# A linear-attention layer fused with a feed-forward layer: one step becomes a 64-token chunk of two batches, with column halves alternating on TensorE and elementwise work taken off GpSimd

## The chip, the cores and the metric

The kernel runs on one core of one Trainium2 chip. Its time is the device time of one execution, in microseconds (us). A core has TensorE (PE in the profile; PEld is its loading of stationary weights), VectorE (DVE), ScalarE (ACT), GpSimd (POOL) and SyncE (SP, which here only starts transfers). Each runs its own instructions in the order in which they were emitted and waits on semaphores for the others.

## The reference

Attention with a decaying state (B = 4 batches, H = 8 heads, S = 768 tokens, head size D = 48), then a feed-forward layer on the 3072 tokens of 384 features, with 2048 hidden features and the gate h * tanh(softplus(h)):

```python
    state = np.zeros((B, H, D, D), dtype=np.float32)
    for t in range(S):
        kt, vt, rt = (k[:, :, t], v[:, :, t], r[:, :, t])
        cur = np.einsum('bhd,bhe->bhde', u[None] * kt, vt)
        y[:, :, t] = np.einsum('bhd,bhde->bhe', rt, state + cur)
        state = w[None, :, :, None] * state + np.einsum('bhd,bhe->bhde', kt, vt)
...
    h = x @ w_in
    sp = np.where(h > 20.0, h, np.log1p(np.exp(np.minimum(h, 20.0))))
    g = h * np.tanh(sp)
    return (g @ w_out).astype(np.float32)
```

The two feed-forward weights arrive as float64.

## The kernel before

**Attention.** The recurrence is done in chunks of C = 64 tokens. A step `s` is two chunks (index `c`) of one batch for all heads; there are 24 steps, six a batch. Heads go in four pairs (`p`) of an even and an odd head (`par`). For a step `load_step` and `load_v` fetch r, k and v; `scale` multiplies r and k by powers of w (L365, L374, into `G`), `diag` makes the u term (L385, L389, L394, L400), `keys` the decayed keys (L418, into `KI`). `scores` multiplies r by k (L435, tile `pa`), and `attend` puts the masked scores into `G` (L459). `chunk` then does, for one chunk, the output y (L496, tile `yt`) and the state for the next chunk (L505, tile `st`), which L518 copies from PSUM into `Wt`, where v lies. So chunk 1 needs chunk 0's state, and a step needs that of the step before it, except at the start of a batch. Each loop over `p` writes y into one half of the output rows (`c * C`), and a state product into rows 0 to 47 or 64 to 111. `finish` copies y out (L527), transposes it (L548) and splits it into two parts of few bits, `xh` and `xl` (L539, L541).

**Weights.** There are 16 tiles of 128 x 768 float64 weights. `convert` makes float32 of their bits (L296 to L312; L312 is an integer add on POOL) and splits the result into two parts (L318, L320).

**Feed-forward.** The tokens go in 8 groups of three steps (384 tokens). For each of 16 f-tiles (128 hidden features) of a group, `up` does 9 matmuls into tile `hp` and `down` 9 into `acc`, all at L572. The `hp` tiles are copied out (L669), and four together form a batch: sigmoid, arctan and sin on ACT (L602 to L608), then gate and split (L613 on DVE, L616 on ACT, L619 on DVE), two f-tiles at a time. Down of a tile follows `LAG` = 9 tiles behind its up. At the end of a group three tiles are copied out (L638) and stored.

**Order.** A planner (`Flow`) emits the instructions. Every piece of work is a generator that says which engines its next instruction may go to and how long it would take there, and the planner sends it where it would be ready first. `dve`, `pool`, `act` and `pe` are its costs. The attention of group g is put into the feed-forward of group g - 1: `place` gives the f-tile behind which a step's four pieces (scores, chunk 0, chunk 1, transposes) may come. Where the plan leaves PE idle, `keep_warm` inserts matmuls on zeros.

Of the kernel before, what the change touches and what calls it, by code (L numbers as in the profile page):

```python
# [23 lines left out]
C = 64  # L24
ST = 2 * C
NST = S // ST
# [25 lines left out]
LAG = 9  # L52
LO0, HI0, LO1, HI1 = 0.05, 0.9, 0.1, 0.75
# [3 lines left out]
# how much a microsecond of an engine counts, and when the engines and tables are there for the stream  # L57
COST = dict(dve=2)
# [67 lines left out]
def dve(cols, fast=False):  # L126
    return {"dve": 0.067 + cols / (1920 if fast else 960)}


def pool(cols):  # L130
    return {"pool": 0.13 + cols / 470}


def act(cols):
    return {"act": 0.03 + cols / 1120}
# [7 lines left out]
def rwkv_mish_kernel(ctx, tc, rkT, rkN, vN, wT, uN, w_in, w_out, consts, rkF, vF, wF, uF, outT):  # L143
# [29 lines left out]
    # persistent double buffers, of which some rows stay zero  # L173
# [7 lines left out]
    for par in range(2):  # L181
        nc.gpsimd.memset(Wt[0][DROWS[par], par, 0], 0.0)
# [6 lines left out]
    # powers of w: TR[., i] = w^(i-32), TK[., j] = w^(31-j), TKn[j, .] = w^(95-j)  # L189
# [53 lines left out]
    doubled(nc.gpsimd, TR, slice)  # L243
# [4 lines left out]
    engines = {"dve": nc.vector, "pool": nc.gpsimd}  # L248
# [3 lines left out]
    def check_range():  # L252
        # whether every w is in the range of these tables
# [17 lines left out]
    # A slot holds a tile of weights as it comes, float64, or its two parts.  # L271
# [10 lines left out]
    def convert(c):  # L282
        """Float64 weights as float32, rounded to nearest, from their bits: the upper word gives
        sign, exponent and 20 bits; the lower one is added to them as a number. Then the two parts."""
        v = nc.vector
        yield f"raw{c}"
        if c >= WE_BUFS:
            yield f"half{c - WE_BUFS}"
        raw = raws.pop(c)
        up, low = raw[:, :, 1], raw[:, :, 0]  # L290
        x, r = up.bitcast(F32), low.bitcast(F32)
# [3 lines left out]
        if engine == "act":  # L295
            nc.scalar.activation(e, x, AF.Abs)  # L296
# [5 lines left out]
        v.tensor_scalar(out=eu, in0=eu, scalar1=3, scalar2=None, op0=ALU.logical_shift_left)  # L302
        yield dve(WE)
        v.scalar_tensor_tensor(out=up, in0=up, scalar=0x80000000, in1=eu, op0=ALU.bitwise_and, op1=ALU.bitwise_xor)
        engine = yield {**act(WE), **dve(WE, True)}
        if engine == "act":
            nc.scalar.activation(r, low, AF.Copy, bias=2.0, scale=2.0**-51)
        else:
            v.tensor_scalar(out=r, in0=low, scalar1=2.0**-51, scalar2=2.0, op0=ALU.mult, op1=ALU.add)
        flow.set(f"half{c}")  # L310
        yield {"pool": 2.1}
        nc.gpsimd.tensor_tensor(out=up.bitcast(I32), in0=up.bitcast(I32), in1=low.bitcast(I32), op=ALU.add)  # L312
        flow.set(f"whole{c}")
# [4 lines left out]
        nc.scalar.copy(out=w[:, 0], in_=x)  # L318
        engine = yield {**dve(WE), **pool(WE)}
        engines[engine].tensor_tensor(out=w[:, 1], in0=x, in1=w[:, 0].bitcast(F32), op=ALU.subtract)  # L320
# [4 lines left out]
    NS = B * NST  # L325
# [4 lines left out]
    def load_step(s):  # L330
        b, i = divmod(s, NST)
# [6 lines left out]
        nc.sync.dma_start(rk[:112], rkT[b, i])  # L338
# [3 lines left out]
        nc.sync.dma_start(n, rkN[b, i])  # L342
# [3 lines left out]
    def load_v(s):  # L346
        b, i = divmod(s, NST)
        if s >= 2:
            yield f"state{s - 2}"
        yield {"sp": 0.55}  # L350
        for par in range(2):
            nc.sync.dma_start(Wt[s % 2][TROWS[par], par], vN[b, i, par])
        if i == 0 and s:
            for par in range(2):
                yield {"pool": 0.2}
                nc.gpsimd.memset(Wt[s % 2][DROWS[par], par, 0], 0.0)
        flow.set(f"v{s}")

    def scale(s):
# [4 lines left out]
        engine = yield {**pool(512), **dve(512)}  # L364
        engines[engine].tensor_tensor(  # L365
# [3 lines left out]
        if s >= 2:  # L369
            yield f"x{s - 2}"  # L370
        for par in range(2):
            r = DROWS[par]
            engine = yield {**pool(512), **dve(512)}
            engines[engine].tensor_tensor(  # L374
# [4 lines left out]
    def diag(s):  # L379
# [4 lines left out]
        engine = yield {**pool(384), **dve(384)}  # L384
        engines[engine].tensor_tensor(  # L385
            out=t1, in0=t1, in1=un.unsqueeze(1).broadcast_to([128, 2, NP, D]), op=ALU.mult
        )
        engine = yield {**pool(384), **dve(384)}
        engines[engine].tensor_tensor(out=t1, in0=t1, in1=n[:, 1], op=ALU.mult)  # L389
# [5 lines left out]
        if s >= 2:  # L395
            yield f"x{s - 2}"
        for par in range(2):
            r = TROWS[par]
            engine = yield {**pool(410), **dve(512)}
            engines[engine].tensor_tensor(  # L400
# [7 lines left out]
    def keys(s):  # L408
# [4 lines left out]
        if s >= 2:  # L413
            yield f"state{s - 2}"
        for par in range(2):
            r = TROWS[par]
            engine = yield {**pool(384), **dve(384)}
            engines[engine].tensor_tensor(  # L418
# [25 lines left out]
    def attend(s):  # L444
        q = s % 2
        yield f"scaled{s}"
        if s:
            yield f"masked{s - 1}"
            if s > GROUPS[0]:
                yield f"state{s - 1}"  # L450
        yield from paced(s, 0)
        yield pe(1.3)
        pa = scores(s)
        flow.set(f"scores{s}")
        yield f"diag{s}"
# [9 lines left out]

    def outputs(s):
        yield f"masked{s}"
# [7 lines left out]
        for c in range(2):  # L475
            yield from paced(s, 1 + c)
            yield from chunk(s, c)
        flow.start(finish(s), rank(s) - L_FIN)

    ys = {}  # L480

    def chunk(s, c):
        q = s % 2
        early = s < GROUPS[0]
        last = c == 1 and s % NST == NST - 1
        yield pe(0.4 if last else (1.35, 0.9)[c])
        if c == 0:
            y = ps.tile([128, 512], F32, name="yt", tag="yt")
            st = [ps.tile([128, 512], F32, name="st", tag=f"{'acc' if early else 'pa'}{par}") for par in range(2)]
            ys[s] = y, st  # L490
        y, st = ys[s]
        for par in range(2):
            k = slice(0, (128, 112)[par])
            for p in range(NP):
                h = 2 * p + par
                nc.tensor.matmul(  # L496
                    y[c * C : (c + 1) * C, h * D : (h + 1) * D],
                    lhsT=G[q][k, par, c, p, :],
                    rhs=Wt[q][k, par, c, p, :],
                    start=True,  # L500
                    stop=True,
                )
            if not last:
                for p in range(NP):
                    nc.tensor.matmul(  # L505
                        st[par][DROWS[par], p * D : (p + 1) * D],
                        lhsT=KI[q][k, par, c, p, :],
# [4 lines left out]
        if not last:  # L512
            nq, ncx = (q, 1) if c == 0 else ((s + 1) % 2, 0)
            for par in range(2):
                r = DROWS[par]
                src = st[par][r, : NP * D].rearrange("d (p e) -> d p e", e=D)
                engine = yield {**act(200), **dve(200)}
                (nc.scalar.copy if engine == "act" else nc.vector.tensor_copy)(out=Wt[nq][r, par, ncx], in_=src)  # L518
        if c == 1:
            flow.set(f"state{s}")  # L520

    def finish(s):
        g = group[s]
        y = ys.pop(s)[0]
        yield act(384)
        ysb = G[s % 2][:, 1].rearrange("a c p i -> a (c p i)")[:, :DM]
        nc.scalar.copy(out=ysb, in_=y[:, :DM])  # L527
        flow.set(f"y{s}")
        if s == starts[g]:
# [360 lines left out]
```

## Time and profile before

| | |
|---|---|
| median of 3 runs | 609.29 us (609.12 to 612.25) |
| profiled execution | span 608.9 us from the first to the last instruction; the page gives no other time for it, and the nearest run is 0.2 us longer |
| TensorE busy | 564.8 us (93%) |
| weight load busy | 534.2 us (88%) |
| VectorE busy | 392.7 us (64%) |
| ScalarE busy | 395.5 us (65%) |
| GpSimd busy | 209.2 us (34%) |
| mean granted TensorE clock | 0.954 |
| moved | HBM 37.98 MB read, 4.72 MB written |

A busy engine is not yet a bound: the shares are means over stages. The slices and stretches shown below say when each engine is full. In the timeline rows stand the start, the time, the engine, the line, the operation, the tile written and those read, shapes, and a count. In the groups stand a line's busy time, the mean of one instruction in ns, and the idle time of the engine ahead of them with what ended it.

### The profile page before, as it was taken

How to read it: one execution, taken by the hardware profiler on the slowest of the kernel's cores; microseconds unless marked ns; L12 is line 12 of the kernel's file. 1: busy time of each engine (PE TensorE's matmuls, PEld its weight loads, DVE VectorE, ACT ScalarE, POOL GpSimd, SP SyncE). 2: the span in 40 equal slices, each digit the busy share in tenths (PEclk: the TensorE clock that was granted, in tenths of full speed). 3: DMA queues.
4: the chain of work that ended last, by engine and by line, in shares of the span. 5: the costliest groups of instructions: out<-in, count | busy, mean ns of one | idle time of the engine just before them, and what ended most of it. 6: DMA issues, size and time to landing. Idle time of an engine off the chain costs nothing. (4 is left out here: it accounts for less than half of the span.)

```text
span 608.9 us, 11432 instructions
## 1 busy us (share of the span) xinstructions
PE 564.8 (93%) x4810; PEld 534.2 (88%) x4810; DVE 392.7 (64%) x502; ACT 395.5 (65%) x478; POOL 209.2 (34%) x167
## 2 busy tenths in 40 slices
PE   7778767779899999999999999999999999999994
PEld 5667766669799999999999999999999999999994
DVE  5999989999768346754756376736684465132332
ACT  4456774648665874766766775587467757678871
POOL 6655588665654113420336033403332120000000
PEclk8798858889799999999999999999999999999998
DMA  8893512011123012301131022302230101000101
GB/s 245 294 373 119 160 57 64 20 57 49 35 70 110 1 57 71 109 14 57 44 105 46 1 70 78 100 2 70 71 103 7 58 15 40 1 0 2 40 0 44
DMA packets 16620, 43.53 MB, mean 71 GB/s; under 512 B 2352, under 2 KB 8752, under 8 KB 16560
## 3 DMA queue, kind: packets, MB, share of 16 engines
q1 hardware_dynamic: 12800, 37.76, 19.6%
q10 hardware_dynamic: 3760, 4.95, 2.3%
q8 instruction: 40, 0.66, 0.4%
q14 instruction: 20, 0.16, 0.1%
HBM read 37.98 MB, written 4.72 MB: 70 GB/s over the span
## 5 line engine op out<-in xcount | busy, mean ns | idle before, releaser
L572 PE MATMUL hp<-xh,w 128*128 128x384 f32 x768 | 225.7, 350 | 2.2 <-DVE hb L669 2.2
L572 PE MATMUL acc<-gh,w 128*128 128x384 f32 x768 | 220.6, 343 | 0.3 <-ACT gh L616 0.3
L572 PEld LDWEIGHTS hp<-xh,w 128*128 128x128 f32 x768 | 143.8, 192 | 5.2 <-DVE hb L669 2.6
L572 PEld LDWEIGHTS acc<-gh,w 128*128 128x128 f32 x768 | 142.8, 191 | 1.9 <-ACT gh L616 0.7
L572 PE MATMUL hp<-xl,w 128*128 128x384 f32 x384 | 131.3, 342 | 2.0 <-DVE xl L541 2.0
L572 PE MATMUL acc<-gl,w 128*128 128x384 f32 x384 | 130.6, 340 | 0.5 <-DVE gl L619 0.5
L669 ACT COPY hb<-hp 128x384 f32<-128x384 f32 x99 | 47.1, 476 | 84.1 <-PE hp L572 83.5
L496 PEld LDWEIGHTS yt<-Wt,G 128*64 128x64 f32 (+1 forms) x768 | 55.2, 147 | 37.0 <-issue 13.4
L613 DVE TENSOR_TENSOR hb<-hb,fa 128x768 f32<-128x768 f32 x64 | 66.3, 1060 | 32.3 <-ACT fa L608 32.3
L496 PE MATMUL yt<-Wt,G 128*64 128x48 f32 (+1 forms) x768 | 63.6, 235 | 23.9 <-DVE G L459 9.9
L572 PEld LDWEIGHTS hp<-xl,w 128*128 128x128 f32 x384 | 74.1, 193 | 2.3 <-DVE xl L541 2.3
L572 PEld LDWEIGHTS acc<-gl,w 128*128 128x128 f32 x384 | 73.4, 191 | 0.8 <-DVE gl L619 0.8
L616 ACT CAST gh<-hb 128x768 fp32r<-128x768 f32 x64 | 51.9, 836 | 33.4 <-DVE hb L613 33.3
L385 POOL TENSOR_TENSOR rkn<-rkn,un 128x384 f32<-128x384 f32 x17 | 20.1, 1182 | 155.0 <-DMA rkn<-in_rkN_dram 155.0
L619 DVE TENSOR_TENSOR gl<-hb,gh 128x768 fp32r<-128x768 f32 x64 | 65.5, 1046 | 10.3 <-ACT gh L616 9.6
L669 DVE COPY hb<-hp 128x384 f32<-128x384 f32 x29 | 16.1, 556 | 65.3 <-PE hp L572 65.2
L400 POOL TENSOR_TENSOR G<-cst,sd 64x512 f32<-64x512 f32 x35 | 46.6, 1331 | 21.0 <-PE t L548 11.0
L505 PE MATMUL st<-Wt,KI 112*48 112x48 f32 (+1 forms) x704 | 51.0, 219 | 0.0
L602 ACT ACTIVATE fa<-hb,bias_ln 128x1536 f32<-128x1536 f32 x32 | 50.5, 1579 | 0.4
L608 ACT ACTIVATE fa<-fa 128x1536 f32<-128x1536 f32 x32 | 47.6, 1487 | 0.4
L605 ACT ACTIVATE fa<-fa 128x1536 f32<-128x1536 f32 x32 | 47.6, 1488 | 0.3
L608 ACT ACT_TABLE_LOAD x32 | 41.1, 1283 | 0.9 <-ACT ob L638 0.4
(70 smaller groups left out, 691.0 us busy)
## 6 DMA issues: line engine op xcount, KB each, us to landing
rk<-in_rkT_dram SPq DMA_DIRECT2D x24, 448.0 KB, 4.1
rkn<-in_rkN_dram SPq DMA_DIRECT2D x24, 384.0 KB, 4.5
wraw<-in_w_in_dram SPq DMA_DIRECT2D x8, 768.0 KB, 8.8
wraw<-in_w_out_dram SPq DMA_DIRECT2D x8, 768.0 KB, 6.8
Wt<-in_vN_dram SPq DMA_DIRECT2D x48, 96.0 KB, 2.4
out_dram<-ob ACTq DMA_DIRECT2D x24, 192.0 KB, 1.9
cst<-in_consts_dram ACTq DMA_DIRECT2D x1, 128.0 KB, 4.7
un<-in_uN_dram ACTq DMA_DIRECT2D x2, 48.0 KB, 4.6
```

Of the source, the lines that this page charges most:

```text
L385: engines[engine].tensor_tensor(out=t1, in0=t1, in1=un.unsqueeze(1).broadcast_to([128, 2, NP, D]), op=ALU.mult)
L400: engines[engine].tensor_tensor(out=G[q][r, par], in0=ident2[r].unsqueeze(1).broadcast_to([C, 2 * NP, C]).rearrange("j (c p) i -> j c p i" ...
L496: nc.tensor.matmul(y[c * C : (c + 1) * C, h * D : (h + 1) * D], lhsT=G[q][k, par, c, p, :], rhs=Wt[q][k, par, c, p, :], start=True, stop=True,
L505: nc.tensor.matmul(st[par][DROWS[par], p * D : (p + 1) * D], lhsT=KI[q][k, par, c, p, :], rhs=Wt[q][k, par, c, p, :], start=True, stop=True,)
L572: nc.tensor.matmul(out, lhsT=a, rhs=m, start=first and n == 0, stop=last and n == 2)
L602: nc.scalar.activation(o.g, o.hb, AF.Sigmoid, bias=bias_ln2, scale=1.0)
L605: nc.scalar.activation(o.g, o.g, AF.Arctan)
L608: nc.scalar.activation(o.g, o.g, AF.Sin, scale=2.0)
L613: nc.vector.tensor_tensor(out=o.hb[:, j], in0=o.hb[:, j], in1=o.g[:, j], op=ALU.mult)
L616: nc.scalar.copy(out=o.gh[:, j], in_=o.hb[:, j])
L619: nc.vector.tensor_tensor(out=o.gl[:, j], in0=o.hb[:, j], in1=o.gh[:, j].bitcast(F32), op=ALU.subtract)
L669: (nc.scalar.copy if engine == "act" else nc.vector.tensor_copy)(out=o.hb[:, j], in_=h)
```

## The change

- **Steps.** A step is now one chunk of two batches (`i, q = divmod(s, NQ)`): index `c` in the tiles is the batch of the pair. Steps s and s + 1 are independent; s + 2 needs the state of s.
- **Products.** `outputs` does all y products of a step, with `c` innermost, so that output rows 0 to 63 and 64 to 127 alternate; then all state products into one PSUM tile, with `par` innermost, so that rows 0 to 47 and 64 to 111 alternate. One copy for each `par` (384 columns) takes the state into `Wt`, where there were two of 192.
- **Insertions.** A step has two pieces instead of four. The transposes of step s - 1 go ahead of the scores of step s (`joined`), except at the ends of groups.
- **GpSimd** keeps memsets. `scale`, `diag`, `keys`, the integer add, the weight split and the table TR go to DVE. The conversion works in the buffer `e` rather than in the raw tile, and a tile starts when the split two tiles earlier is done; the conversion of the low word is always on ACT.
- **Planner.** `LAG` 9 becomes 8; the costs of DVE, ACT and PE and the places of the pieces change.

Lines move by up to ten in the changed file: y is L484, the state L497, its copy L510, the transposes L550, the feed-forward L574, the integer add L307, the weight split L314, `xl` L543, the gate L615 and L621.

```diff
-LAG = 9
-LO0, HI0, LO1, HI1 = 0.05, 0.9, 0.1, 0.75
+LAG = 8
+LO0, HI0, LO1, HI1 = 0.05, 0.9, 0.05, 0.8
...
-    doubled(nc.gpsimd, TR, slice)
+    doubled(nc.vector, TR, slice)
...
         if c >= WE_BUFS:
-            yield f"half{c - WE_BUFS}"
+            yield f"split{c - WE_BUFS}"
...
+        yield act(WE)
+        nc.scalar.activation(r, low, AF.Copy, bias=2.0, scale=2.0**-51)
         yield dve(WE)
-        v.scalar_tensor_tensor(out=up, in0=up, scalar=0x80000000, in1=eu, op0=ALU.bitwise_and, op1=ALU.bitwise_xor)
...
-        yield {"pool": 2.1}
-        nc.gpsimd.tensor_tensor(out=up.bitcast(I32), in0=up.bitcast(I32), in1=low.bitcast(I32), op=ALU.add)
+        v.scalar_tensor_tensor(out=eu, in0=up, scalar=0x80000000, in1=eu, op0=ALU.bitwise_and, op1=ALU.bitwise_xor)
+        yield dve(WE)
+        v.tensor_tensor(out=e.bitcast(I32), in0=e.bitcast(I32), in1=r.bitcast(I32), op=ALU.add)
...
-            engine = yield {**pool(512), **dve(512)}
-            engines[engine].tensor_tensor(
+            yield dve(512)
+            nc.vector.tensor_tensor(
                 out=G[q][r, par], in0=rk[r, 0], in1=TR[r].unsqueeze(1).broadcast_to([D, 2, NP, C]), op=ALU.mult
             )
...
+        joined = s and group[s] == group[s - 1] and group[s]
+        if joined:
+            yield f"y{s - 1}"
         yield from paced(s, 0)
-        yield pe(1.3)
+        yield pe(1.6 if joined else 1.25)
+        t = turned(s - 1) if joined else None
         pa = scores(s)
...
-        for c in range(2):
-            yield from paced(s, 1 + c)
-            yield from chunk(s, c)
...
+        for p in range(NP):
+            for par in range(2):
+                k = slice(0, (128, 112)[par])
                 h = 2 * p + par
+                for c in range(2):
                     nc.tensor.matmul(
+                        y[c * C : (c + 1) * C, h * D : (h + 1) * D],
+                        lhsT=G[q][k, par, c, p, :],
                         rhs=Wt[q][k, par, c, p, :],
...
         if not last:
+            for c in range(2):
+                for p in range(NP):
+                    for par in range(2):
+                        k = slice(0, (128, 112)[par])
+                        n = (c * NP + p) * D
+                        nc.tensor.matmul(
+                            st[DROWS[par], n : n + D],
...
-        at = (4 * (s - starts[g]) + piece) / (4 * GROUPS[g])
+        at = (2 * (s - starts[g]) + piece) / (2 * GROUPS[g])
```

PE in the dense part, before, from the last up matmuls ahead of chunk 0 of a step to the first down matmuls behind it (an instruction here is one matmul of the program):

```order
L572 MATMUL hp<-xl,w 128x384
L572 MATMUL hp<-xh,w 128x384
L496 MATMUL yt<-Wt_88,G_86 64x48 x4
L505 MATMUL st<-Wt_88,KI_90 48x48 x4
L496 MATMUL yt<-Wt_88,G_86 64x48 x4
L505 MATMUL st<-Wt_88,KI_90 48x48 x4
L572 MATMUL acc_1765<-gh,w 128x384
```

PE in the same part after the change, from the last down matmuls ahead of a step's outputs to the first up matmuls behind them:

```order
L574 MATMUL acc_1754<-gl,w 128x384
L574 MATMUL acc_1754<-gh,w 128x384
L484 MATMUL yt<-Wt_88,G_86 64x48 x16
L497 MATMUL st<-Wt_88,KI_90 48x48 x16
L574 MATMUL hp<-xh,w 128x384
L574 MATMUL hp<-xl,w 128x384
```

Before, a second insertion of the same four rows follows one down block later; now all 32 products of a step stand in one place.

POOL before, early in the program, with the conversion of weights and the preparation of steps 3 to 5:

```order
L312 TENSOR_TENSOR wraw<-wraw 128x768 x2
L374 TENSOR_TENSOR G_86<-rk,TR 48x512
L418 TENSOR_TENSOR KI_90<-rkn,TKn 64x384
L400 TENSOR_TENSOR G_86<-cst,sd 64x512
L374 TENSOR_TENSOR G_85<-rk,TR 48x512
L385 TENSOR_TENSOR rkn<-rkn,un 128x384
L374 TENSOR_TENSOR G_85<-rk,TR 48x512
L389 TENSOR_TENSOR rkn<-rkn 128x384
L320 TENSOR_TENSOR w<-wraw,w 128x768
```

DVE after the change in the like place, up to the split of a weight tile (`ISA` is the integer add, over 1536 half-words):

```order
L407 TENSOR_TENSOR KI_90<-rkn,TKn 64x384
L305 SCALAR_TENSOR_TENSOR we<-wraw,we 128x768
L383 TENSOR_REDUCE sd<-rkn 128x8
L307 ISA we<-wraw,we 128x1536
L543 TENSOR_TENSOR xl<-t,xh 128x3x128
L453 COPY_PREDICATED G_85<-cst,pa_878 64x512
L314 TENSOR_TENSOR w<-we,w 128x768
L453 COPY_PREDICATED G_85<-cst,pa_879 64x512
L363 TENSOR_TENSOR G_86<-rk,TR 48x512
L389 TENSOR_TENSOR G_86<-cst,sd 64x512
L363 TENSOR_TENSOR G_86<-rk,TR 48x512
L389 TENSOR_TENSOR G_86<-cst,sd 64x512
```

What POOL did beside DVE stands now in DVE's own queue, between the masks (L453) that PE waits for and the splits that up tiles wait for.

More of the change, by code (lines that the diff above doesn't have):

```diff
@@ L24 @@
 C = 64
+NQ = B // 2
+NC = S // C
+NS = NC * NQ
 ST = 2 * C
-NST = S // ST
 DM, DFF = H * D, 2048
@@ L56 @@
 DMA_LAT = 2.0
-COST = dict(dve=2)
+COST = dict(dve=1.5)
 FREE = dict(pe=10.0, act=9.0, dve=7.9, pool=9.0, sp=0.5)
@@ L180, in rwkv_mish_kernel @@
             nc.gpsimd.memset(a[i][32:64, 0], 0.0)
-    for par in range(2):
-        nc.gpsimd.memset(Wt[0][DROWS[par], par, 0], 0.0)
+    for i in range(2):
+        for par in range(2):
+            nc.gpsimd.memset(Wt[i][DROWS[par], par], 0.0)
     ET = mybir.EngineType
@@ L346, in load_v @@
     def load_v(s):
-        b, i = divmod(s, NST)
+        i, q = divmod(s, NQ)
         if s >= 2:
-            yield f"state{s - 2}"
+            yield f"out{s - 2}"
         yield {"sp": 0.55}
         for par in range(2):
[L352 to L356, printed above, removed]
+            nc.sync.dma_start(Wt[q][TROWS[par], par], vN[i, q, par])
         flow.set(f"v{s}")
@@ L383, in diag @@
         t1 = n[:, 0]
-        engine = yield {**pool(384), **dve(384)}
-        engines[engine].tensor_tensor(
+        yield dve(384)
+        nc.vector.tensor_tensor(
             out=t1, in0=t1, in1=un.unsqueeze(1).broadcast_to([128, 2, NP, D]), op=ALU.mult
         )
-        engine = yield {**pool(384), **dve(384)}
-        engines[engine].tensor_tensor(out=t1, in0=t1, in1=n[:, 1], op=ALU.mult)
+        yield dve(384)
+        nc.vector.tensor_tensor(out=t1, in0=t1, in1=n[:, 1], op=ALU.mult)
         if s >= 2:
@@ L413, in keys @@
         if s >= 2:
-            yield f"state{s - 2}"
+            yield f"out{s - 2}"
         for par in range(2):
             r = TROWS[par]
-            engine = yield {**pool(384), **dve(384)}
-            engines[engine].tensor_tensor(
+            yield dve(384)
+            nc.vector.tensor_tensor(
                 out=KI[q][r, par],
@@ L464, in attend @@
         flow.set(f"masked{s}")
+    ys = {}
     def outputs(s):
+        q = s % 2
+        early = s < GROUPS[0]
+        last = s >= NS - NQ
         yield f"masked{s}"
@@ L474, in outputs @@
                 yield f"x{s - 1}"
-        for c in range(2):
-            yield from paced(s, 1 + c)
-            yield from chunk(s, c)
[L478 to L494, printed above, removed]
-                h = 2 * p + par
[L496 to L504, printed above, removed]
+        yield from paced(s, 1)
+        yield pe(1.1 if last else 2.0)
+        y = ps.tile([128, 512], F32, name="yt", tag="yt")
+        st = ps.tile([128, 512], F32, name="st", tag="acc0" if early else "pa0")
+        for p in range(NP):
+            for par in range(2):
+                k = slice(0, (128, 112)[par])
+                h = 2 * p + par
+                for c in range(2):
                     nc.tensor.matmul(
-                        st[par][DROWS[par], p * D : (p + 1) * D],
-                        lhsT=KI[q][k, par, c, p, :],
+                        y[c * C : (c + 1) * C, h * D : (h + 1) * D],
+                        lhsT=G[q][k, par, c, p, :],
                         rhs=Wt[q][k, par, c, p, :],
@@ L512, in chunk, with evacuate_y, turned, finish @@
         if not last:
-            nq, ncx = (q, 1) if c == 0 else ((s + 1) % 2, 0)
+            for c in range(2):
+                for p in range(NP):
+                    for par in range(2):
+                        k = slice(0, (128, 112)[par])
+                        n = (c * NP + p) * D
+                        nc.tensor.matmul(
+                            st[DROWS[par], n : n + D],
+                            lhsT=KI[q][k, par, c, p, :],
+                            rhs=Wt[q][k, par, c, p, :],
+                            start=True,
+                            stop=True,
+                        )
+        flow.set(f"out{s}")
+        flow.start(evacuate_y(s, y), rank(s) - L_FIN)
+        if not last:
             for par in range(2):
                 r = DROWS[par]
[L516 to L524, printed above, removed]
+                engine = yield {**act(384), **dve(384)}
+                (nc.scalar.copy if engine == "act" else nc.vector.tensor_copy)(
+                    out=Wt[q][r, par].rearrange("d c p e -> d (c p e)"), in_=st[r, : 2 * NP * D]
+                )
+        flow.set(f"state{s}")
+    def evacuate_y(s, y):
+        if s:
+            yield f"turned{s - 1}"
         yield act(384)
-        ysb = G[s % 2][:, 1].rearrange("a c p i -> a (c p i)")[:, :DM]
+        ys[s] = ysb = G[s % 2][:, 1].rearrange("a c p i -> a (c p i)")[:, :DM]
         nc.scalar.copy(out=ysb, in_=y[:, :DM])
         flow.set(f"y{s}")
+        if s + 1 == NS or group[s + 1] != group[s] or not group[s]:
+            yield from paced(s, 2)
+            yield pe(0.36)
+            flow.start(finish(s, turned(s)), rank(s) - L_FIN)
+    def turned(s):
+        t = transposes(ys.pop(s), "acc2" if s < GROUPS[0] else "yt")
+        flow.set(f"turned{s}")
+        return t
+    def finish(s, t):
+        g = group[s]
         if s == starts[g]:
@@ L713, in down_tile @@
                 for mt in range(KT):
-                    yield f"out{g - 1},{mt}"
+                    yield f"put{g - 1},{mt}"
             else:
@@ L730, in output @@
         put(engine, mt, T, slice(starts[g] * 128, starts[g] * 128 + T))
-        flow.set(f"out{g},{mt}")
+        flow.set(f"put{g},{mt}")
     def ffn():
```

78 lines of the change are left out of this document (36 added, 42 removed).

## Prediction

> **What bounds the kernel now.** I read the page first: which engine is full, and when.
>
> ```profile
> PE 564.8 (93%) x4810; PEld 534.2 (88%) x4810; DVE 392.7 (64%) x502; ACT 395.5 (65%) x478; POOL 209.2 (34%) x167
> ...
> PE   7778767779899999999999999999999999999994
> ...
> DVE  5999989999768346754756376736684465132332
> ...
> POOL 6655588665654113420336033403332120000000
> ```
>
> There are two regimes. From about slice 10 (a slice is 15.2 us) TensorE (PE) is full; before that PE has gaps and VectorE (DVE) is full, with GpSimd (POOL) busy beside it. The stage view puts numbers on both.
>
> ```profile
> 0.00:50.00 50.00, 38.33 (x420) 31.50 (x420) 42.78 (x64) 23.53 (x47) 29.98 (x35) 0.84 0.85 298
> 50.00:100.00 50.00, 37.12 (x272) 34.02 (x272) 46.74 (x55) 31.67 (x38) 36.64 (x21) 0.81 0.28 85
> 100.00:141.50 41.50, 32.43 (x290) 29.90 (x290) 40.19 (x45) 24.15 (x34) 28.39 (x21) 0.89 0.18 53
> 300.00:400.00 100.00, 100.00 (x914) 95.36 (x913) 62.59 (x83) 66.03 (x80) 32.56 (x27) 1.00 0.22 66
> ```
>
> After the stretch come PE, weight load, DVE, ACT and POOL busy time, the granted clock, and DMA. Up to 141.5 us DVE is busy for 42.78 + 46.74 + 40.19 = 129.7 us; from 300 to 400 PE never stops and DVE has 37 us to spare. I cut at 141.5 because there the second group's feed-forward starts (its first matmul is the second row below):
>
> ```profile
> 141.29 0.34 PE L572 MATMUL acc<-gh,w 128*128 128x384 f32 x1
> 141.46 0.34 PE L572 MATMUL hp<-xh,w 128*128 128x384 f32 x1
> ...
> 601.43 0.34 PE L572 MATMUL acc<-gh,w 128*128 128x384 f32 x1
> ```
>
> The last matmul ends at 601.43 + 0.34 = 601.8, and the span is 608.9: a tail of 7.1 us for three copies and their stores. So span = 141.5 (DVE's regime) + 460.3 (PE's) + 7.1. I predict each part.
>
> **PE's regime: what an insertion costs.** In the timeline of PE, an inserted piece of attention costs the distance between the last feed-forward matmul before it and the second one behind it, less two normal steps. [...]
>
> ```profile
> 264.31 0.33 PE L572 MATMUL hp<-xl,w 128*128 128x384 f32 x1
> ...
> 282.68 0.34 PE L572 MATMUL acc<-gh,w 128*128 128x384 f32 x1
> 282.95 1.15 PE L435 MATMUL pa<-G,rk 48*64 48x64 f32 x32
> 284.03 0.45 PE L572 MATMUL hp<-xh,w 128*128 128x384 f32 x1
> 284.31 0.34 PE L572 MATMUL hp<-xl,w 128*128 128x384 f32 x1
> ...
> 288.65 0.34 PE L572 MATMUL hp<-xh,w 128*128 128x384 f32 x1
> 288.91 0.67 PE L496 MATMUL yt<-Wt,G 128*64 128x48 f32 x8
> 289.42 0.52 PE L505 MATMUL st<-Wt,KI 128*48 128x48 f32 x8
> ...
> 290.07 0.22 PE L496 MATMUL yt<-Wt,G 112*64 112x48 f32 x1
> 290.09 0.21 PE L505 MATMUL st<-Wt,KI 112*48 112x48 f32 x1
> 290.13 0.22 PE L496 MATMUL yt<-Wt,G 112*64 112x48 f32 x1
> ...
> 290.79 0.33 PE L572 MATMUL acc<-gl,w 128*128 128x384 f32 x1
> ...
> 292.00 0.34 PE L572 MATMUL acc<-gh,w 128*128 128x384 f32 x1
> ...
> 294.00 0.34 PE L572 MATMUL hp<-xl,w 128*128 128x384 f32 x1
> ```
>
> The normal step: from 264.31 to 282.68 lie 106 steps, 173.3 ns each, so a block of nine takes 1.56 us. Scores: 284.31 - 282.68 - 0.35 = 1.28 us for 32 matmuls (the program's 16, each of two passes). They start over 284.03 - 282.95 = 1.08 us, 34 ns apiece; the other 0.2 us is the price of inserting at all. Chunk 0: 290.79 - 288.65 - 0.35 = 1.79 us. Chunk 1: 294.00 - 292.00 - 0.35 = 1.65 us. So y and state cost 3.44 us a step.
>
> Why so much, the rows inside chunk 0 tell. Eight y that write one column half take 289.42 - 288.91 = 0.51 us, 64 ns each. Where y (rows 0 to 63 of its output) and the odd state product (64 to 111) alternate, a pair takes 290.13 - 290.07 = 0.06 us, about 28 ns apiece. Two column halves run beside each other, although both use the same 112 contraction rows.
>
> The change alternates halves in every y and every state product: 64 matmuls in one insertion. At 28 ns that is 1.8 + 0.2 = 2.0 us; at the scores' 34 ns, 2.4. I take 2.0, since the 28 ns are those of these very products. Its open point: in the quoted pair the two outputs lie in different PSUM tiles, now in one (all y in yt, all state in pa0), which no row shows. If that undoes the overlap, 64 times 64 ns + 0.2 = 4.3 us is the upper bound.
>
> [...]
>
> Behind 141.5 us lie 18 steps: before, 18 x 1.79 + 15 x 1.65 + 3 batch ends of 16 y alone (16 x 64 ns + 0.2 = 1.2) = 60.6 us. After, 16 x 2.0 + 2 final steps of y alone (32 x 28 ns + 0.2 = 1.1) = 34.2 us. **Saved: 26.4 us.** Scores and transposes keep their matmuls; joining them in 12 places could save at most 12 x 0.2 = 2.4 us and is taken as nothing.
>
> **LAG 8.** One down block lies ahead of the second group's start instead of behind it: minus 1.6 us here, and plus 1.6 at the end, where the last gating chain is covered by five down blocks instead of six. Net zero.
>
> **Lost time in PE's regime.** 460.3 us less 233 blocks x 1.56 (363.4), 60.6 and 18 x (1.28 + 0.33 for transposes) = 29.0 leaves 7.3 us lost before. PE misses 0.9 us of it in one stretch at the end (next row), where the last gate is awaited. For after I take 6: the end 0.9 + 1.6 = 2.5, the rest 3.5. What could grow is the gating chain:
>
> ```profile
> 590.00:600.00 10.00, 9.12 (x51) 8.54 (x50) 3.65 (x4) 4.11 (x4) 0.00 (x0) 1.00 0.01 2
> ```
>
> ```profile
> 273.38 1.82 DVE L619 TENSOR_TENSOR gl<-hb,gh 128x768 fp32r<-128x768 f32 x2 [0.78 <-ACT gh L616]
> 276.61 0.34 PE L572 MATMUL hp<-xh,w 128*128 128x384 f32 x1
> ```
>
> This gate ends at 275.2, and the up tile that reuses its buffer starts at 276.6: 1.4 us to spare where no large insertion covers it. A group has one such place after the change too, and six groups that are 2 us late each would lose 12 us. DVE's load does not force it: a group's 3 steps need, by the prices below, 15 x 0.69 + 15 x 0.55 + 3 x 0.55 + 6 x 0.73 + 16 gates x 0.95 + 5 copies x 0.55 = 43 us of about 61 (32 blocks, 3 x 3.6 of attention).
>
> **DVE's regime: GpSimd's work at DVE's price.** Two groups of the same gate, first up to 141.5 us, then from 500 to 600 where POOL is idle:
>
> ```profile
> L613 DVE TENSOR_TENSOR hb<-hb,fa 128x768 f32<-128x768 f32 x6 | 8.1, 1383 | 0.0
> ...
> L613 DVE TENSOR_TENSOR hb<-hb,fa 128x768 f32<-128x768 f32 x14 | 12.8, 952 | 15.5 <-ACT fa L608 15.5
> ```
>
> Beside a working POOL the same instruction takes 1383 ns instead of 952. POOL's 95 us up to 141.5 were thus partly paid by DVE. The clean prices stand in a stretch with POOL idle, and in one at 113 us:
>
> ```profile
> 113.92 0.69 DVE L374 TENSOR_TENSOR G<-rk,TR 48x512 f32<-48x512 f32 x1
> ...
> 136.60 0.95 DVE L304 SCALAR_TENSOR_TENSOR wraw<-wraw,we 128x768 uint32<-128x768 uint32 x1
> 137.47 0.55 DVE L385 TENSOR_TENSOR rkn<-rkn,un 128x384 f32<-128x384 f32 x1
> 137.94 0.55 DVE L300 TENSOR_SCALAR we<-we 128x768 f32<-128x768 f32 x1
> 138.41 0.55 DVE L389 TENSOR_TENSOR rkn<-rkn 128x384 f32<-128x384 f32 x1
> ```
>
> In the new order DVE has, up to the split of step 5 (L543, which opens the second group): 37 products of 512 columns x 0.69 = 25.5; 38 of 384 x 0.55 = 20.9; 25 of 768 x 0.95 = 23.8; 14 three-operand ones x 0.95 = 13.3; 33 single-input ones x 0.55 = 18.2; 12 masked copies x 0.73 = 8.8; 8 reductions and 3 PSUM copies x 0.55 = 6.1; 26 table and other small ones, about 4; and 13 integer adds (L307), new on DVE. For their price the program gives 1536 half-words; as 768 words an add costs 0.95 like its neighbours, and at one half-word a cycle, by the slope from 0.69 (512) to 0.95 (768), about 1.75. I take 0.95, 12.4 us, because the instruction has the byte count of a 768-column one; the other end adds 10.4.
>
> The sum is 133 us. Instructions that are queued start 0.47 apart though they last 0.55 (the three rows above); half of some 200 gaining 0.06 to 0.08 takes off 6. DVE's first table operation can start at about 6.5 us, as now. Without waits the split comes at 133.5. Waits are what DVE hardly has now (129.7 busy of 141.5). When it is faster it will meet ACT and PE: the masks behind the scores of the first steps, the first gate behind four feed-forward tiles and three activations, the gates of the next batches. I put 9 us on it, bounded by 3 and 18. **Start of the second group: 143 us (before 141.5); 137 to 152, with dear adds to 160.** The tables' extra doubling (TR on DVE, 7 small ones) is in the sum; the four memsets on POOL are early and hide behind the first loads; SP's loads keep their number and their bytes; ACT's six more word conversions hide, as ACT is busy 24 to 32 us of 50.
>
> **The sum**: 608.9 + 1.5 (start) - 26.4 - 1.6 (block moved ahead) - 1.3 (lost 7.3 to 6) = 581.1. The median of the runs, 609.29, is 0.4 above this span: **581.5, rounded to 582 us.**
>
> **Rivals.**
> 1. The adds run one half-word a cycle, or ACT holds DVE up for 18 us: start at 152 to 154, 591 to 593 us. For it: no row shows the add on DVE. Against: ACT is half idle there.
> [...]
> 3. The chain with 1.4 us to spare breaks: 2 us in each of six groups, 594 us.
> 4. The early regime really shrinks (waits of 3): 576 us; with a cheaper join, 573.
>
> The change may also not do what it says on POOL; the order shows only memsets left there, so I give that nothing.
>
> [...]
>
> **How the numbers follow.** Likeliest case 0.58, by itself 576 to 588; rival 1 0.16; rival 2 0.06; rival 3 0.10; rival 4 0.08; both 1 and 3 or worse, 600 to 612, 0.02. The range goes from the lower end of rival 4 to the upper of 1 and 3 with the 34 ns pace (16 x 0.4 = 6 us more): 572 to 599, leaving out about 0.12. About 0.5% (3 us) is what a measurement here can tell from none. Faster 0.92, same 0.02, slower 0.06.
>
> **What would show it.** Right: in PE's timeline y and state in one stretch of some 1.8 us; DVE's gates at 0.95 us from the start; the second group's first up tile near 143 us; PE full from there. Wrong: y starts 60 ns apart (rival 2); L307 at 1.7 us (rival 1); PE idle ahead of up tiles with DVE's gl as releaser (rival 3). A start after 160 us, or several us lost in each group, would break the forecast.

## The result and the profile after

| | median | runs | against before |
|---|---|---|---|
| before | 610.02 us | 609.12 to 612.25 (4) | |
| after | 583.07 us | 582.20 to 588.28 (4) | 0.957, 95% interval 0.952 to 0.961 |

The change makes the kernel 27 us faster. The forecast was 582 us, range 572 to 599. The profiled execution took 582.2 us with a span of 580.3.

The page of the kernel after: totals, then slices (now 14.5 us each).

```profile
PE 525.2 (90%) x4825; PEld 500.8 (86%) x4825; DVE 388.0 (67%) x594; ACT 406.5 (70%) x490; POOL 4.2 (1%) x15
...
PE   7994473876999999999999999999999999999994
...
DVE  5996998899878755775577558846875654324332
...
POOL 2000000000000000000000000000000000000000
```

PE has lost 40 us of busy time with about as many matmul records (4825 for 4810). Of these, 30 us lie behind the start of the second group's feed-forward (456.9 us busy before, 426.7 now), where the same work overlaps more. The two regimes remain. The stretches of the kernel after (columns as before):

```profile
0.00:50.00 50.00, 44.01 (x542) 36.95 (x542) 42.02 (x89) 21.68 (x44) 4.24 (x15) 0.97 0.95 332
50.00:100.00 50.00, 21.43 (x240) 19.02 (x241) 43.48 (x68) 29.70 (x35) 0.00 (x0) 0.65 0.27 74
100.00:141.50 41.50, 29.86 (x222) 27.34 (x220) 36.51 (x55) 27.48 (x35) 0.00 (x0) 0.85 0.09 26
300.00:400.00 100.00, 100.00 (x940) 96.70 (x939) 66.35 (x98) 75.30 (x88) 0.00 (x0) 1.00 0.20 63
```

Up to 141.5 us DVE is busy for 122.0 us: less than the 129.7 of before, although all of POOL's products and adds are now its own. Groups of DVE up to 145 us show why:

```profile
L307 DVE CUSTOM_DVE_ANT_0 we<-wraw,we 128x1536 uint16<-128x1536 uint16 x14 | 13.1, 951 | 0.3 <-ACT wraw L303 0.2
...
L615 DVE TENSOR_TENSOR hb<-hb,fa 128x768 f32<-128x768 f32 x6 | 5.6, 954 | 1.4 <-ACT fa L610 1.4
```

The integer add costs 951 ns, and the gate has fallen from 1383 to 954 ns. The timeline of PE around an insertion in the dense part, and the start of the second group's feed-forward:

```profile
144.67 0.34 PE L574 MATMUL hp<-xh,w 128*128 128x384 f32 x1
...
248.52 0.34 PE L574 MATMUL acc<-gh,w 128*128 128x384 f32 x1
248.79 1.14 PE L484 MATMUL yt<-Wt,G 128*64 128x48 f32 x32
249.76 0.89 PE L497 MATMUL st<-Wt,KI 128*48 128x48 f32 x32
250.58 0.44 PE L574 MATMUL hp<-xh,w 128*128 128x384 f32 x1
250.86 0.34 PE L574 MATMUL hp<-xl,w 128*128 128x384 f32 x1
...
573.65 0.34 PE L574 MATMUL acc<-gh,w 128*128 128x384 f32 x1
```

By the prediction's measure (up to the second matmul behind it, since the first lasts 0.44 us instead of 0.34) the insertion costs 250.86 - 248.52 - 0.35 = 1.99 us. The 32 y start over 249.76 - 248.79 = 0.97 us (30 ns apiece), the 32 state products over 0.82 (26 ns).

So the span divides as follows ("start" is the first matmul of the second group's feed-forward, "dense" the time from there to the last matmul's end):

| | start | dense | tail | span |
|---|---|---|---|---|
| before | 141.5 | 460.3 | 7.1 | 608.9 |
| after, predicted | 143 | 431.0 | 7.1 | 581.1 |
| after | 144.7 | 429.3 | 6.3 | 580.3 |

The dense part carries the gain, 31.0 us; the start gives 3.2 back.

### The profile page after: what moved, and what is told of

The parts are those of the page before. It is cut to its first block, busy times and chain, and to the rows that moved or that the text cites. A ratio compares the mean times of both kernels' runs of the same rounds, so it can differ in the third digit from the quotient of the medians.

```text
span 580.3 us, 11242 instructions
## 1 busy us (share of the span) xinstructions
PE 525.2 (90%) x4825; PEld 500.8 (86%) x4825; DVE 388.0 (67%) x594; ACT 406.5 (70%) x490; POOL 4.2 (1%) x15
## 5 line engine op out<-in xcount | busy, mean ns | idle before, releaser
L574 PE MATMUL hp<-xh,w 128*128 128x384 f32 x768 | 225.7, 349 | 29.3 <-ACT w L312 21.3
L574 PE MATMUL acc<-gh,w 128*128 128x384 f32 x768 | 217.8, 339 | 2.0 <-ACT gh L618 1.9
L574 PEld LDWEIGHTS hp<-xh,w 128*128 128x128 f32 x768 | 143.5, 192 | 34.3 <-ACT w L312 22.1
L574 PEld LDWEIGHTS acc<-gh,w 128*128 128x128 f32 x768 | 141.6, 189 | 3.5 <-ACT gh L618 2.2
L574 PE MATMUL hp<-xl,w 128*128 128x384 f32 x384 | 131.3, 342 | 0.0
L574 PE MATMUL acc<-gl,w 128*128 128x384 f32 x384 | 129.6, 338 | 0.6 <-DVE gl L621 0.6
L671 ACT COPY hb<-hp 128x384 f32<-128x384 f32 x110 | 52.1, 474 | 66.2 <-PE hp L574 56.5
L453 DVE COPY_PREDICATED G<-cst,pa 64x512 f32<-64x512 uint32 x48 | 35.2, 733 | 70.4 <-PE pa L424 69.6
L574 PEld LDWEIGHTS hp<-xl,w 128*128 128x128 f32 x384 | 74.0, 193 | 0.0
L574 PEld LDWEIGHTS acc<-gl,w 128*128 128x128 f32 x384 | 72.9, 190 | 0.8 <-DVE gl L621 0.8
L615 DVE TENSOR_TENSOR hb<-hb,fa 128x768 f32<-128x768 f32 x64 | 58.8, 950 | 19.9 <-ACT fa L610 19.9
L621 DVE TENSOR_TENSOR gl<-hb,gh 128x768 fp32r<-128x768 f32 x64 | 59.3, 953 | 3.4 <-ACT gh L618 2.5
L520 ACT COPY G<-yt 128x384 f32<-128x384 f32 x24 | 11.5, 479 | 39.7 <-PE yt L484 39.7
L424 PEld LDWEIGHTS pa<-G,rk 48*64 48x64 f32 x768 | 25.5, 138 | 13.3 <-DVE G L363 8.7
L424 PE MATMUL pa<-G,rk 48*64 48x64 f32 x768 | 29.2, 225 | 8.1 <-DVE G L363 8.1
L484 PEld LDWEIGHTS yt<-Wt,G 128*64 128x64 f32 (+1 forms) x768 | 25.5, 141 | 12.0 <-DVE G L453 6.4
## 6 DMA issues: line engine op xcount, KB each, us to landing
rk<-in_rkT_dram SPq DMA_DIRECT2D x24, 448.0 KB, 4.0
```

The source lines that it names most:

```text
L424: nc.tensor.matmul(pa[par][TROWS[par], n : n + C], lhsT=rk[r, 1, c, p, :], rhs=G[q][r, par, c, p, :], start=True, stop=True,)
L453: nc.vector.copy_predicated(out=G[q][r, par].rearrange("j c p i -> j (c p) i"), mask=mask[r].unsqueeze(1).broadcast_to([C, 2 * NP, C]), da ...
L484: nc.tensor.matmul(y[c * C : (c + 1) * C, h * D : (h + 1) * D], lhsT=G[q][k, par, c, p, :], rhs=Wt[q][k, par, c, p, :], start=True, stop=True,
L574: nc.tensor.matmul(out, lhsT=a, rhs=m, start=first and n == 0, stop=last and n == 2)
L615: nc.vector.tensor_tensor(out=o.hb[:, j], in0=o.hb[:, j], in1=o.g[:, j], op=ALU.mult)
L621: nc.vector.tensor_tensor(out=o.gl[:, j], in0=o.hb[:, j], in1=o.gh[:, j].bitcast(F32), op=ALU.subtract)
```

## The experiments

All times are medians, with the ratio to the kernel before timed on the same chip (its median lay between 610.8 and 611.0 us). Start and dense come from the one profiled execution of each version. Two executions of the same order of work had starts 6 us apart (last section), so a smaller difference between two starts shows nothing by itself; there the medians count.

| run | median | ratio, 95% interval | start | dense |
|---|---|---|---|---|
| y halves in blocks | 597.97 | 0.979 (0.976 to 0.981) | 149.1 | 443.4 |
| y and state halves in blocks | 607.55 | 0.995 (0.992 to 0.998) | 146.8 | 448.0 |
| two insertions | 592.82 | 0.971 (0.969 to 0.973) | 144.9 | 440.5 |
| before, without GpSimd | 612.45 | 1.002 (1.001 to 1.004) | 142.9 | 460.8 |
| after, GpSimd back | 585.16 | 0.959 (0.955 to 0.963) | 141.7 | 434.3 |
| LAG 9 | 584.04 | 0.956 (0.954 to 0.958) | 141.9 | 434.2 |
| early loads | 589.71 | 0.964 (0.961 to 0.967) | 151.1 | 430.6 |
| early loads, LAG 9 | 589.14 | 0.964 (0.961 to 0.968) | 145.2 | 436.1 |
| planner's dearer loads | 583.13 | 0.955 (0.953 to 0.957) | 144.0 | 430.1 |
| early loads, later rank | 577.41 | 0.946 (0.944 to 0.949) | 138.6 | 430.6 |
| small last parts | 584.41 | 0.955 (0.952 to 0.958) | 150.7 | 429.8 |
| early v, small last parts | 573.30 | 0.940 (0.938 to 0.942) | 134.0 | 429.7 |

### Is it the alternation?

The matmuls stay the same, and the insertions too; only the order inside changes. First y, one half of the output rows after the other:

```diff
-        for p in range(NP):
-            for par in range(2):
+        for c in range(2):
+            for p in range(NP):
+                for par in range(2):
...
-                for c in range(2):
                     nc.tensor.matmul(
                         y[c * C : (c + 1) * C, h * D : (h + 1) * D],
```

> Theory (the alternation of the column halves pays): the 32 passes of the y products again run in two blocks of one half each, at the 64 ns that a pass of y took in one half before, instead of a pair every 58 ns; less a few passes that overlap where the blocks meet. y takes 1.6 to 2.0 us instead of 0.93, an insertion costs 2.6 to 3.0 us instead of 1.99, and 18 of them behind the start of the second group's feed-forward make 583 + 11 to 18 = 594 to 601 us. Rival (one insertion in place of two saved the time, the order inside is worth nothing): 583 us, within 2.

Timeline of PE in that kernel at an insertion:

```profile
256.20 0.34 PE L574 MATMUL acc<-gh,w 128*128 128x384 f32 x1
256.47 1.70 PE L484 MATMUL yt<-Wt,G 128*64 128x48 f32 x29
...
258.15 0.91 PE L497 MATMUL st<-Wt,KI 128*48 128x48 f32 x29
258.99 0.45 PE L574 MATMUL hp<-xh,w 128*128 128x384 f32 x1
259.28 0.33 PE L574 MATMUL hp<-xl,w 128*128 128x384 f32 x1
```

The insertion costs 259.28 - 256.20 - 0.35 = 2.73 us, 0.74 more. Over 18 steps that is 13.3 us; the dense part grew by 14.1. Then the state products as well, with `par` as their outermost loop:

```diff
-            for c in range(2):
-                for p in range(NP):
-                    for par in range(2):
+            for par in range(2):
+                for c in range(2):
+                    for p in range(NP):
```

> Theory (alternation): besides y, the 32 passes of the state products run in two blocks at 44 ns a pass as before, 1.3 to 1.4 us instead of 0.72. On top of the run with y in blocks 0.5 to 0.6 us in 16 insertions, 8 to 10 us: 602 to 611 us. Rival (fewer insertions): 583 us, within 2. If a block of the state alone overlaps for a reason other than the halves, it equals the run with y in blocks.

```profile
255.82 0.34 PE L574 MATMUL acc<-gh,w 128*128 128x384 f32 x1
256.09 1.70 PE L484 MATMUL yt<-Wt,G 128*64 128x48 f32 x29
...
257.74 1.33 PE L497 MATMUL st<-Wt,KI 128*48 128x48 f32 x29
259.00 0.44 PE L574 MATMUL hp<-xh,w 128*128 128x384 f32 x1
259.28 0.34 PE L574 MATMUL hp<-xl,w 128*128 128x384 f32 x1
```

Now 3.11 us: the state's share is 0.38, below the 0.5 to 0.6 expected. Dense grows by 18.7 (16 x 1.12 + 2 x 0.74 = 19.4). The median lies 4.5 us above the profiled run, 603.0; no trace shows where those lie. Both are in the expected range, and the rival's 583 is out: the order inside the insertion is worth some 19 us.

### Is it one insertion instead of two?

```diff
-        yield pe(1.1 if last else 2.0)
+        yield pe(1.1)
...
         if not last:
+            yield from paced(s, 1.5)
+            yield pe(0.9)
             for c in range(2):
```

> y and state products stay alternating but go in as two insertions, with feed-forward blocks between them. Theory: an insertion by itself costs about 0.2 us, in 16 steps 3 us: 586 us (584 to 588). Rival (the joining into one insertion is what saved): half of the 26 us comes back, 594 us or more.

It came out between theory and rival. PE's timeline at the two insertions of a step (here L576 is the feed-forward and L499 the state):

```profile
221.50 0.34 PE L576 MATMUL acc<-gh,w 128*128 128x384 f32 x1
221.77 1.14 PE L484 MATMUL yt<-Wt,G 128*64 128x48 f32 x32
...
223.12 0.34 PE L576 MATMUL hp<-xl,w 128*128 128x384 f32 x1
...
225.89 0.34 PE L576 MATMUL acc<-gh,w 128*128 128x384 f32 x1
226.16 0.93 PE L499 MATMUL st<-Wt,KI 128*48 128x48 f32 x32
...
227.30 0.34 PE L576 MATMUL hp<-xl,w 128*128 128x384 f32 x1
```

By the same measure y alone costs 1.27 us and the state alone 1.06, together 0.34 more than 1.99: 16 x 0.34 = 5.4 us. Dense grew by 11.2. The stretch behind the start in that kernel, and in the kernel after below it:

```profile
141.50:200.00 58.50, 56.02 (x543) 52.94 (x542) 48.55 (x73) 43.50 (x51) 0.00 (x0) 0.97 0.20 64
```

```profile
141.50:200.00 58.50, 58.34 (x572) 56.19 (x571) 48.31 (x73) 48.55 (x59) 0.00 (x0) 1.00 0.22 65
```

Another 2.3 us are PE waits here, for weights not yet converted, which the kernel after does not have at this place; most of the rest lies in two places where, behind a stall, some ten matmuls started 0.32 instead of 0.173 us apart (about 1.5 us each); the granted clock of the stretch above is 0.97, that of the kernel after 1.00. So the joining itself is worth 5.4 us, more than the 3 that I had put on it.

The three shares, 0.74 + 0.38 + 0.34 = 1.46 us, add up to the whole fall of the insertion from 3.44 to 1.99.

### Does GpSimd's part bring anything?

The kernel before with its elementwise work on DVE and the conversion of the kernel after:

```diff
-        engine = yield {**pool(512), **dve(512)}
+        engine = yield dve(512)
...
-        yield {"pool": 2.1}
-        nc.gpsimd.tensor_tensor(out=up.bitcast(I32), in0=up.bitcast(I32), in1=low.bitcast(I32), op=ALU.add)
+        yield dve(WE)
+        v.tensor_tensor(out=e.bitcast(I32), in0=e.bitcast(I32), in1=r.bitcast(I32), op=ALU.add)
```

> The kernel before, with its GpSimd work on VectorE and the conversion of the weights as in the kernel after; its two insertions of unalternated products are kept. Theory: GpSimd's work at VectorE's clean prices gives the early regime about the length that it had (start of the second group's feed-forward at 141 to 149 us) and leaves the dense part alone: 607 to 617 us, 612 the likeliest. Rival (that GpSimd no longer slows VectorE is a good share of the gain): 603 us or less.

And the kernel after with the products of `scale`, `diag` and `keys` on either engine (the integer add and the weight split stay on DVE):

```diff
-        yield dve(512)
-        nc.vector.tensor_tensor(
+        engine = yield {**pool(512), **dve(512)}
+        engines[engine].tensor_tensor(
```

> The kernel after with the products of scale, diag and keys free to go to GpSimd again, by the planner's old cost. Theory: in the dense part nothing changes, since VectorE has a third to spare there; in the early regime VectorE loses up to 20 us of products and pays for GpSimd's neighbourhood (a gate 1.38 instead of 0.95 us), so the start of the second group's feed-forward lies between 139 and 149 us: 578 to 588 us, 583 the likeliest. Rival (GpSimd beside VectorE is what made the kernel before slow): over 590 us.

By itself the removal changes next to nothing (1.002). With GpSimd back the start comes 3.0 us earlier, but dense is 5.0 us longer: 2.3 us of PE waits for weights right behind the start, and two stretches of matmuls 0.32 us apart, there (the granted clock from 141.5 to 200 us is 0.97 instead of 1.00) and at the end. In sum 2 us slower than the kernel after, with overlapping intervals. Groups of that kernel up to 141 us:

```profile
L620 DVE TENSOR_TENSOR hb<-hb,fa 128x768 f32<-128x768 f32 x6 | 8.2, 1411 | 0.1
```

The gate (here L620) is back at 1411 ns. In the windows up to the start POOL is busy for 76.2 us, and DVE's busy time is still 125.1 us, as in the kernel after (125.15). DVE has 43 products less there, 26.5 us at the prices of the kernel after; its remaining instructions became 24.2 us dearer. What POOL took over, DVE paid in slower instructions. Behind the start it is the same between the kernels before and after: DVE is busy for 263.0 us with POOL busy for 114.2 beside it, and for 262.8 us with that work its own (ACT is busy for 9 us more there).

### LAG

```diff
-LAG = 8
+LAG = 9
```

> LAG 9 as before. Theory (net zero): one down block more behind the second group's start, 1.6 us, and a wait at the end that is about 1.6 us shorter, since a sixth down block covers the last gating chain: 583 us, within 2. Rival (the shorter lag was a gain of its own): 585 to 587 us.

Same, as expected, but not only by the two expected terms. The start comes 2.8 us earlier and dense is 4.9 longer, of which 1.6 each are the block that moved. Behind the last up tile PE's first interval falls from 2.23 to 0.67 us, as the theory has it. But PE has new waits in the dense part, some 5 us together: y waits in six insertions (five cost 2.30 to 2.85 us instead of 1.99, one of y alone 2.12 instead of 1.27), and two down tiles wait for the copy of the output before them. The theory had none of these.

### Where could the start still gain?

Waits of DVE in the kernel after up to 145 us (total, times, longest):

```profile
DVE wc L191 <- DMA wt<-in_wT_dram: 5.2, 1, 5.2
DVE rkn L374 <- DMA rkn<-in_rkN_dram: 4.2, 1, 4.2
DVE we L299 <- ACT we L295: 2.8, 4, 1.1
```

The second wait is the k of step 3, issued behind four loads of weights.

```diff
-            flow.start(thread(s), rank(s) + k / 1000 - (L_V if group[s] and thread is load_v else 0), 0.0)
+            flow.start(thread(s), s - 600 if thread is load_step else rank(s) + k / 1000 - ..., 0.0)
```

> The loads of r and k of a step go ahead of the loads of weights in SyncE's order as soon as their buffer is free. In the kernel after VectorE waits 4.2 us at 54 us for the k of step 3, queued behind four weight loads. Theory (the early regime is VectorE's): the wait goes and the start comes 3 to 4 us earlier, 579 to 580 us. Rival (weights that land later, or the scores' wait behind, hold it up instead): 583 us, within 1.5.

> The early loads together with LAG 9. If both effects are as the theory has them, the sum of the two runs alone: 579 to 581 us; if LAG 9 only moves a block, it equals the run with early loads within 1.5 us.

Both times miss, and in the wrong direction: 6 us slower. That LAG 9 leaves the time of the early loads where it is (589.1 and 589.7 us) is what the second expectation has for a lag that only moves a block. The first weight tile's clip on DVE, in the kernel after and then with early loads:

```profile
30.89 0.54 DVE L299 TENSOR_SCALAR we<-we 128x768 f32<-128x768 f32 x1
```

```profile
33.62 0.67 DVE L354 TENSOR_TENSOR rk<-rk,TK 112x512 f32<-112x512 f32 x1
...
41.34 0.54 DVE L299 TENSOR_SCALAR we<-we 128x768 f32<-128x768 f32 x1
```

With its data there early, step 3 takes DVE from 33.6 us on, ahead of the conversions; the first up tile comes at 48.8 instead of 41.8 us. The late load had kept step 3 behind the weights. Part of the 10 us by which the clip is late is the clock: from 14 to 24 us its granted mean was 0.66 in this execution, and the first `xl` came at 26.31 instead of 23.58 us. The run with LAG 9 had 1.00 there; its clip comes at 39.80 and its first up tile at 47.2 us, against 31.28 and 42.2 with LAG 9 alone. So the order on DVE delays the weights with or without the slow clock; the 5.9 us between the starts of these two runs are more than the block that LAG moves, and what makes up the rest was not parted. Two runs part load and order. One leaves the loads where they are and only tells the planner that they are slow (`"sp": 2.4` for 2.19, `DMA_LAT` 4 for 2):

> The order of loads is left; only the planner's prices for them are raised to what the trace shows (weights 2.4 us instead of 2.19 on the queue, a load's landing 4 us instead of 2), so that VectorE's order gets the products of step 3 behind the conversion of weights that have landed. Theory (the 4.2 us wait at 54 us is one of order on VectorE, not of the loads): the wait goes, the first up tile stays near 42 us, the start of the second group's feed-forward comes 2 to 4 us earlier: 579 to 581 us. Rival (whatever takes the place of the wait, as with early loads): 583 to 590 us.

The 4.2 us wait is gone, yet the start is at 144.0 and the time 583.1 us, as the rival has it: other waits took its place (4.0 us on ACT's part of the conversion). The other takes the early loads and puts the second group's steps later:

```diff
-        return place(s, 0) - L_ATT if group[s] else s - 1000
+        return place(s, 0) - (L_ATT if group[s] > 1 else 0) if group[s] else s - 1000
```

> The early loads again, with the second group's steps four places later in rank, behind the conversion of the first weights. With early loads alone the first up tile came at 48.8 us instead of 41.8 and the start at 151 instead of 144.7. Theory (the products of step 3 took VectorE ahead of the conversions): first up back at 42 to 45 us and a start of 141 to 146 us, 580 to 585 us. Rival (the loads themselves delay the weights): still 586 to 590 us, with a first up tile at 47 us or later.

577.4 us, better than expected: the start comes at 138.6. Early data and a later order together gain about what early data alone lost; the later rank on the old loads was not run, so that it takes both is not shown. Its trace names the next wait of PE:

```profile
PE yt L484 <- DMA Wt<-in_vN_dram: 11.7, 1, 11.7
```

That is the v of step 3. Before that the end was looked at alone, with parts of one tile in the last gate batch:

```diff
-        n = -(-o.n // GS)
+        n = -(-o.n // (GS if b + 1 < len(GROUPS) * NF // FB else o.n))
```

> The last gate batch in parts of one tile instead of two. Theory (the 2.2 and 1.0 us that TensorE misses behind the last up tile are the last gating chain): the first tile's parts take 0.55 + 0.4 + 0.55 us instead of 0.95 + 0.7 + 0.95, so about 1.1 us of the wait goes: 582 us, and TensorE's last matmul ends 1 us nearer to the start of the dense part. Rival (more instructions on VectorE and ScalarE cost as much): 583 us or more.

The timeline of PE behind the last up tile, in the kernel after and with small parts:

```profile
564.41 0.34 PE L574 MATMUL acc<-gh,w 128*128 128x384 f32 x1
566.64 0.44 PE L574 MATMUL acc<-gh,w 128*128 128x384 f32 x1 [1.89 <-ACT gh L618]
567.64 0.45 PE L574 MATMUL acc<-gl,w 128*128 128x384 f32 x1 [0.56 <-DVE gl L621]
```

```profile
570.31 0.34 PE L574 MATMUL acc<-gh,w 128*128 128x384 f32 x1
571.82 0.45 PE L574 MATMUL acc<-gh,w 128*128 128x384 f32 x1 [1.17 <-ACT gh L618]
572.63 0.44 PE L574 MATMUL acc<-gl,w 128*128 128x384 f32 x1 [0.36 <-DVE gl L621]
```

From the first row to the third it is 3.23 us before and 2.32 now: 0.9 us less, near the 1.1 expected; in the time this is lost in the spread, and the median, 584.4 us, lies on the rival's side. Last, small parts and later rank together, with the v loads of the second group's steps ranked like those of r and k:

```diff
-            flow.start(thread(s), s - 600 if thread is load_step else ...
+            flow.start(thread(s), s - 600 if thread in (load_step, load_v) and group[s] < 2 else s - 600 if thread is load_step else ...
```

> The version with early loads and later rank (577.4 us), with two more edits: the v loads of the second group's steps go ahead of the weights as well (TensorE waited 11.7 us for the v of step 3 there), and the last gate batch in parts of one tile (TensorE's wait at the end went from 2.23 + 1.00 to 1.51 + 0.81 us in the run of that part alone). Theory: PE's 11.7 us was partly on the path of the early regime, start 136 to 138 us instead of 138.6, and 0.5 to 1 us at the end: 574 to 577 us. Rival (VectorE, 118 us busy before the start, was the bound there, and v ahead of the weights delays their conversion): 577 to 584 us.

573.3 us, 0.940 of the kernel before (0.938 to 0.942), 10 us below the kernel after, whose interval lies apart. It is a little better than the range expected, with a start of 134.0 us where 136 to 138 was. (The 118 us of VectorE named there are those up to 134 us of the kernel with early loads and later rank; up to its start it was busy for 121.4.) Stretch up to the start in this kernel, then in the kernel after:

```profile
0.00:134.00 134.00, 96.68 (x1017) 85.53 (x1018) 121.67 (x208) 82.88 (x119) 4.23 (x15) 0.83 0.51 160
```

```profile
0.00:144.67 144.67, 98.47 (x1020) 86.48 (x1020) 125.15 (x214) 80.92 (x116) 4.24 (x15) 0.82 0.45 148
```

DVE has 3.5 us less to do before the start and is idle for 12.3 instead of 19.5 us. How much each of the edits has of this was not parted. It is the fastest version that was run.

## Why the prediction was right, point by point

- **The sum.** The start came 1.7 us later than predicted, the dense part 1.7 us shorter, the tail 0.8 us shorter, and the time outside the span is 1.5 us more: 582.2 us in the profiled execution, for 581.5. That the total is so near is in part luck: the start and the lost time below were off and cancelled. The largest term, the insertions, was right by its mechanism.
- **Insertion, 2.0 us predicted, 1.99 measured.** The one open point, two halves in one PSUM tile, is settled: they overlap there too (30 and 26 ns apiece). The three runs on order and insertion account for the whole saving. The last steps of y alone cost 1.27 instead of 1.1: 32 y at 30 ns and 0.3 us for inserting, where I had taken 28 and 0.2. Sum of insertions 34.4 us (34.2 predicted).
- **The order of the halves.** Blocks of one half cost 0.74 us (y) and 0.38 us (state) more than alternating halves with the same contraction rows: 3.11 against 1.99 us for the same 64 matmuls.
- **Joined transposes** save nothing, as taken: 1.62 us joined, 1.28 + 0.34 apart.
- **Lost time** in the dense part was 3.8 us (429.3 less 232 blocks x 1.56 = 361.9, 34.4 and 29.2 for scores and transposes) against 6 predicted: 2.9 at the end (2.23 + 1.00 - 2 x 0.17; 2.5 predicted, and 2.45 if only PE's idle time is counted) and 0.9 elsewhere. The 3.5 predicted for elsewhere had no row behind it. Some 5.5 of the 7.3 us before lay in one place, a wait of PE for the masks (2.49 us) and the slow matmuls behind it (those of the feed-forward from 159.03 us on start 0.32 instead of 0.173 us apart):

```profile
157.27 0.77 PE L496 MATMUL yt<-Wt,G 112*64 112x48 f32 x5 [2.49 <-DVE G L459]
```

The kernel after has no such wait. The gating chain (rival 3) held: no group lost time on it.

- **LAG 8, net zero**: the two medians lie within 1 us, and the two predicted terms show in the trace. The waits that LAG 9 adds were not foreseen.
- **Start, 143 predicted, 144.7 measured.** Right in size, by two errors that partly cancel: DVE's work was 125.2 us (133 - 6 = 127 predicted), its idle time 19.5 (6.5 + 9 = 15.5). The add's price was right (951 ns for 1536 half-words, beside 950 for its neighbour L305 of 768 words). Of the waits the term that I had not named is the load of step 3's k, 4.2 us; I had said that the loads keep their number and bytes and left their place in the queue out.
- **The tail and the time outside the span.** The tail was 6.3 instead of 7.1 us. Outside the span lie 582.2 - 580.3 = 1.9 us, where I had taken 0.4, the distance of one span to a median of other runs. The two errors go opposite ways in the total and leave 0.7 us.
- Rival 1 is refuted by the row of the add (951 ns), and rival 2, the slower case in which two halves in one PSUM tile do not overlap (4.3 us an insertion), by the rows of y (30 ns apart); rival 4 did not occur, but the last run shows that the early regime can shrink by 10.7 us with other loads and another order.

## What to carry to other kernels

Where many small products follow each other on TensorE, try an order in which neighbours go to different column halves of the output: here the same products cost a third less (1.99 instead of 3.11 us a step), and that was two thirds of this gain. GpSimd beside a busy VectorE brought little here: it took over 26.5 us of products, and VectorE's remaining instructions became 24.2 us dearer. In a stage bound by one engine a late load can do useful ordering: here the loads alone moved forward cost 6 us, and the loads and the rank of the work that they feed, moved together, gained 6.

## What was not expected of the hardware

**The same early regime differs by 6 us between two executions.** The run with small last parts has the kernel after's order on DVE, ACT and SP up to the last gate batch, but its start lies at 150.7 instead of 144.7 us. It begins 14 to 24 us into the span. That stretch in the kernel after and in that run, then a row of PE's timeline of each:

```profile
14.00:24.00 10.00, 9.68 (x178) 8.51 (x177) 9.71 (x17) 3.75 (x6) 0.00 (x0) 1.00 1.02 369
```

```profile
14.00:24.00 10.00, 10.00 (x135) 8.02 (x133) 9.43 (x16) 2.87 (x6) 0.00 (x0) 0.70 1.02 375
```

```profile
15.49 3.34 PE L237 MATMUL idle<-zeros 128*128 128x256 bf16 x29
```

```profile
16.47 5.09 PE L237 MATMUL idle<-zeros 128*128 128x256 bf16 x29
```

The granted clock is 0.70 instead of 1.00, and `keep_warm`'s 29 matmuls on zeros take 5.09 instead of 3.34 us. They lie ahead of the first step's y, and DVE's `xl` behind it comes 1.4 us later. Up to 110 us this grows to 2.5, and by 122 us it is 5.4; from 110 to 134 us the granted clock is 0.79 in that run and 0.91 in the kernel after. The same happens at the end: behind the last gate's wait some ten matmuls start 0.32 instead of 0.173 us apart in eight of the fourteen profiled executions (about 1.5 us; in the run with small last parts from 573.1 to 576.6 us), and do not in the others, those of the kernels before and after among them. It is likely, but not shown, that this is the spread of the times of the kernel after, 582 to 588 us: its slowest run has the lowest granted clock of its four (0.944, the others 0.949 to 0.953), but was not traced. Nor is it on record whether the two traces come from one chip.
